# Later batches' scores in four 64 by 64 quarters of the array, with odd chunks reversed and a new order

## The chip, the cores and the metric

One core of a Trainium2 chip runs the program. A time is the device time of one execution in microseconds. TensorE is called PE, VectorE DVE, ScalarE ACT, GpSimd POOL, and SP issues most of the transfers.

## What is computed

A gated linear attention over four batches of eight heads, 768 tokens and 48 features per head, then a Fourier mixing and a feed-forward network (FFN), everything in f32:

```python
for t in range(S):                       # S = 768, per head, D = 48
    state = alpha[t][:, None] * state + outer(k[t], v[t])
    y[t] = q[t] @ state
x = y, heads side by side                # 768 tokens x 384
u = x + real(fft(fft(x, axis=tokens), axis=features))
un = layernorm(u)
out = u + relu(un @ w_ch1) @ w_ch2       # 384 -> 1536 -> 384
```

## The kernel before

**Attention.** Each of the four batches has four pairs of heads (a "unit"). The first head of a pair sits in partitions 0 to 63 (48 used, the rest zero), the second in partitions 64 to 111. The 768 tokens are cut into six chunks of 128. Stage s1 makes running products of the decays by two scans on DVE: A, in a tile of the tag "w3" (printed as w), and its backward counterpart, in the tile al itself. s2 and s3 (`times`) multiply the keys into al and the queries into A. s4 transposes the keys by PE into kt. s5 makes the scores of each chunk: keys as stationary operand, queries as moving operand, so that the output has keys in rows and queries in columns; one matmul per chunk and head, the two heads in the two row halves of the array. A query sees only keys up to its own time, so the lower half of each 128 by 128 block has to be zero. In batch 0 DVE masks while it copies out of PSUM; in batches 1 to 3 (`scores`) ACT copies three chunks at a time to an X tile of the tag w3, and POOL writes the zeros with `affine_select`. The states of the chunks (s6, `states` and `moves`) run on PE, DVE and ACT. s7 (`reads`) multiplies X by the values vn and adds the earlier state's part; two output halves of 64 tokens go to the two column halves of the array. `take` copies the result to y by ACT.

**Mixing, normalising, FFN.** The mixing (folds on DVE, token and feature transforms on PE, a gather of reversed rows through DRAM by POOL) and the normalising give the x tiles. Then an FFN of two blocks per batch runs, each block as 12 slices: nine matmuls of 128x384 into an "f1" bank of PSUM (`mk1`), ACT's relu and DVE's remainder out of it, and nine matmuls into three "f2" banks (`mk2`).

**The order.** The program writes down operations with keys, and a planner (class `Plan`) puts them in order by a model: on each engine the ready operation with the lowest key first. The dictionary `PLACE` replaces single keys by others. An FFN operation is a fill with a late key, so that the attention of batch b+1 goes ahead of the FFN of batch b whenever it is ready. Where the plan leaves PE empty in the first 220 us, warming matmuls on zeros are put in (line 1460, before the change; these are all the records f<-zero). PSUM has three banks "a", two "f1" and three "f2"; there are five w3 tiles, four al tiles and two kq tiles. One scores stage takes three banks a, one bank f1 and two w3 tiles at once. All operations of the plan are recorded by one line, 616, but relu (294) and the warming matmuls (1460).

Of the kernel before, what the change touches and what calls it, by code (L numbers as in the profile page):

```python
# [17 lines left out]
ALU = mybir.AluOpType  # L18
AX = mybir.AxisListType

B, H, S, D = 4, 8, 768, 48
DM = H * D
DFF = 4 * DM
P = 128
NT = S // P
NP2 = H // 2
# [6 lines left out]
GRP = 64  # L33
NV = 64
VW = NT * H // NP2 * D + 32
# [107 lines left out]
THALF = (slice(0, GRP), slice(GRP, P))  # L143
HEADS = ((0, slice(0, GRP)), (1, slice(GRP, CW)))
# [58 lines left out]
def real(x):  # L203
# [5 lines left out]


PLACE = {
# [22 lines left out]
}  # L234


# [17 lines left out]
class Plan:  # L254


    def __init__(self, engines):
        self.engines, self.ops, self.tags, self.direct, self.key, self.chain, self.fill = engines, [], {}, None, 0.0, None, False
        self.idle, self.open, self.both, self.half, self.tight, self.mode, self.run = None, set(), None, None, False, None, None
        self.read, self.last, self.after = {}, None, None  # L260

    def tag(self, name, count, make, reals=None):
        reals = reals or [make(i) for i in range(count)]
# [34 lines left out]
    def add(self, engines, name, args, kwargs):  # L298
# [5 lines left out]
        op = Op(engines, fns, args, kwargs, self.key if self.fill else PLACE.get(round(self.key, 3), self.key))  # L304
        n = len(self.ops)
# [4 lines left out]
        for k, a in named:  # L310
            if isinstance(a, Rows):
                a = a.view
# [10 lines left out]
                    x.tile.uses += 1  # L323
            self.both = None
        op.slots.sort(key=lambda x: x.index if x.tag else -1)
        op.name, op.half, op.mode, op.follows = name, None, None, False
        if name == "matmul":
            p0, p1 = self.region(args[1])[0:2]
            op.half = p0 if p1 - p0 <= GRP else None
# [134 lines left out]
    def emit(self):  # L464
# [35 lines left out]
        while placed < len(ops):  # L500
            placed += 1
            best = None
            for e, cand in wait.items():
# [6 lines left out]
                for n in cand:  # L510
                    op = ops[n]
                    t = start(op, e)
# [18 lines left out]
                n, t = pick  # L531
# [10 lines left out]
            op.engine, op.dur = engine, op.durs[engine]  # L542
            if engine == "PE":
                lead = n + 1 if n + 1 < len(ops) and ops[n + 1].follows else None
                if op.half == GRP and self.half == 0:
                    op.dur = 0.005
                elif op.mode != self.mode:
                    op.dur += max(SWITCH[op.mode], SWITCH[self.mode])
                self.half, self.mode = op.half, op.mode
# [83 lines left out]


@with_exitstack
def gla_mix_ffn(ctx: ExitStack, tc: tile.TileContext, alpha, kq, v, w1, w2, consts, tables, rowtab, out):
    nc = tc.nc
    plan = Plan({"PE": nc.tensor, "ACT": nc.scalar, "DVE": nc.vector, "POOL": nc.gpsimd, "SP": nc.sync})
    V, A, G, T, SY = (Engine(plan, e) for e in ("DVE", "ACT", "POOL", "PE", "SP"))
# [113 lines left out]
    def load_rest(p):  # L753
        if p < B * NP2:
            if p in (2, 3):
                if p == 2:
                    loaded["lent"] = plain(plan.tile("wt11"))
                t = plain(plan.tile(f"wt{7 + p}")).rearrange("p (two s) -> p two s", two=2)
                vn = loaded["lent"][:, (p - 2) * VW : (p - 1) * VW]
            else:  # L760
                t, vn = plan.tile("kq"), plan.tile("vn")
            loaded["kq", p] = t
            loaded["vn", p] = vn
            SY.dma_start(t, kq[p])
            SY.dma_start(vn, v[p, :, 0:VW])

    def setup():
        V.memset(zero, 0.0)
# [53 lines left out]
    def attn_stages(b, hp, i, mixed):  # L822
# [20 lines left out]
            )  # L843

        def R(rows, c):
            return loaded["al", pair][rows, c * CP + 2 : c * CP + 2 + P]

        def Aq(rows, c):
            return e["A"][rows, c * CP + 1 : c * CP + 1 + P]

        def times(which, x, o, c0, c1):
            y = span(x[0:CW], c0, c1, o)
            k = loaded["kq", pair][0:CW, which, c0 * P : c1 * P].rearrange("p (c t) -> p c t", t=P)
            FL["mul"].tensor_mul(y, k, y)

        parts = ((0, 3), (3, NT)) if pair == 0 else ((0, NT),)
# [51 lines left out]
        def scores():  # L908
            tiles = [w3() for _ in range(2)]
            X = [x[:, 0:S].rearrange("p (c n) -> p c n", c=NT) for x in tiles]  # L910
            e["X"] = X
            pc = [[psa() for _ in range(2)], [psa(), plan.tile("f1")]]
            plan.both = pc[0] + pc[1] + tiles
            plan.run = []
            for c in range(NT):
                for hd, r in HEADS:
                    T.matmul(pc[c // 3][hd][:, c % 3 * P : (c % 3 + 1) * P], R(r, c), Aq(r, c), start=True, stop=True)
            plan.run = None
            for h2 in range(2):
                for hd in range(2):  # L920
                    xs = X[hd][:, 3 * h2 : 3 * h2 + 3].rearrange("p c n -> p (c n)")
                    FL["ev"].copy(xs, pc[h2][hd][:, 0:DM])
                    G.affine_select(out=xs, in_=xs, pattern=[[0, 3], [1, P]], compare_op=ALU.is_ge, fill=0.0, base=0, channel_multiplier=-1)

        def s6():
            states()
# [642 lines left out]
def layout(q, k, v, alpha, moe_w_ch1, moe_w_ch2):  # L1569


    def pairs(x, fill):
        t = np.full((B * NP2, P, S), fill, np.float32)
        h = x[:, HORD].reshape(B * NP2, 2, S, D).transpose(0, 1, 3, 2)
        t[:, 0:D], t[:, GRP:CW] = h[:, 0], h[:, 1]
        return t

    decay = np.zeros((B * NP2, P, AW), np.float32)
    decay[..., 0 : NT * CP].reshape(B * NP2, P, NT, CP)[..., 1:] = pairs(alpha, 1.0).reshape(B * NP2, P, NT, P)
    v = v[:, HORD]  # L1580
    v = np.stack([x[..., ::-1] if h >= H // 2 else x for h, x in zip(HORD, v.swapaxes(0, 1))], axis=1)
    values = np.zeros((B * NP2, P, VROW), np.float32)
    values[..., 0 : NT * 2 * D] = v.reshape(B * NP2, 2, NT, P, D).transpose(0, 3, 2, 1, 4).reshape(B * NP2, P, NT * 2 * D)
    return {
        "alpha": decay, "kq": np.stack([pairs(k, 0.0), pairs(q, 0.0)], axis=2), "v": values,
        "w1": np.ascontiguousarray(moe_w_ch1[FEAT]).view(np.int64), "w2": np.ascontiguousarray(moe_w_ch2[:, FEAT]).view(np.int64),
        "consts": dft_constants(), "tables": first_tables(), "rowtab": row_table() - DM,
    }
# [27 lines left out]
```

## Time and profile before

| what | us |
|---|---|
| median of 3 runs (lowest to highest) | 480.93 (478.38 to 482.18) |
| the profiled execution | 478.37 |
| its span, first to last instruction | 476.7 |
| PE busy in it | 468.4 |
| DVE busy | 321.5 |
| ACT busy | 203.0 |
| POOL busy | 53.0 |

The profiled execution lies 1.7 us above its span, and 2.6 us under the median. A matmul's record lasts longer than the time by which it moves the next one on, because matmuls are pipelined: what a stage costs PE is read from the starts, not from the busy time. A matmul with both operands in f32 leaves two records, one in fp32r or a transposition leaves one.

### The profile page before, as it was taken

How to read it: one execution, taken by the hardware profiler on the slowest of the kernel's cores; microseconds unless marked ns; L12 is line 12 of the kernel's file. 1: busy time of each engine (PE TensorE's matmuls, PEld its weight loads, DVE VectorE, ACT ScalarE, POOL GpSimd, SP SyncE). 2: the span in 40 equal slices, each digit the busy share in tenths (PEclk: the TensorE clock that was granted, in tenths of full speed). 3: DMA queues.
4: the chain of work that ended last, by engine and by line, in shares of the span. 5: the costliest groups of instructions: out<-in, count | busy, mean ns of one | idle time of the engine just before them, and what ended most of it. 6: DMA issues, size and time to landing. Idle time of an engine off the chain costs nothing.

```text
span 476.7 us, 10695 instructions
## 1 busy us (share of the span) xinstructions
PE 468.4 (98%) x4546; PEld 444.5 (93%) x4546; DVE 321.5 (67%) x623; ACT 203.0 (43%) x410; POOL 53.0 (11%) x70
## 2 busy tenths in 40 slices
PE   9999999999999999999999999999999999999995
PEld 8979689999999999999999999999999999999994
DVE  7999889999868989657289976583184833113112
ACT  3486759748593234445432254333412251111110
POOL 0000300105113000304120001231130000000000
PEclk9999999999999999999999999999999999999999
DMA  8998215123636201215272001200040001001001
GB/s 304 405 396 322 75 34 191 51 87 133 260 94 180 65 1 51 80 48 194 95 231 77 3 0 51 94 8 22 1 151 1 0 1 51 0 1 50 1 0 56
DMA packets 20981, 46.05 MB, mean 97 GB/s; under 512 B 1920, under 2 KB 11008, under 8 KB 20800
## 3 DMA queue, kind: packets, MB, share of 16 engines
q1 hardware_dynamic: 19872, 42.81, 25.5%
q0 software_dynamic: 768, 2.37, 2.0%
q8 instruction: 37, 0.61, 0.5%
q10 hardware_dynamic: 288, 0.13, 0.1%
q14 instruction: 16, 0.13, 0.1%
HBM read 38.22 MB, written 7.08 MB: 95 GB/s over the span
## 4 chain that ended last, share of the span: by engine, by line
PE 92%; DVE 4%; issue 1%; DMA 1%; ACT 1%; DVEq 0%; ACTq 0%
PE f L616 67%; PE a L616 21%; PE f L1460 4%; DVE al L616 1%; DVE w L616 1%; DVE x L616 1%; DMA al<-in_alpha_dram 1%; DVE tc L616 1%; DVE y L616 0%; ACT b L616 0%; ACT h L294 0%; ACT tt L616 0%; ACT kt L616 0%; DVE back L616 0%; DVE zero L616 0%
## 5 line engine op out<-in xcount | busy, mean ns | idle before, releaser
L616 PE MATMUL f<-wt,h 128*128 128x384 f32 x864 | 173.5, 340 | 0.4 <-ACT h L294 0.4
L616 PE MATMUL f<-x,wt 128*128 128x384 f32 x864 | 171.5, 339 | 0.0
L616 PEld LDWEIGHTS f<-wt,h 128*128 128x128 f32 x864 | 149.4, 188 | 2.6 <-ACT h L294 0.9
L616 PEld LDWEIGHTS f<-x,wt 128*128 128x128 f32 x864 | 150.0, 188 | 1.9 <-issue 0.3
L616 DVE SCALAR_TENSOR_TENSOR h<-f,h 128x384 fp32r<-128x384 f32 x96 | 53.3, 555 | 109.4 <-ACT h L294 108.3
L294 ACT ACTIVATE h<-f 128x384 fp32r<-128x384 f32 x96 | 47.3, 492 | 159.2 <-PE f L616 157.9
L616 POOL TENSOR_SCALAR_AFFINE_SELECT w<-w 128x384 f32<-128x384 f32 x48 | 37.1, 806 | 222.7 <-ACT w L616 222.7
L616 DVE TENSOR_TENSOR y<-y,a 128x191 f32<-128x191 f32 (+3 forms) x65 | 24.5, 427 | 10.4 <-PE a L616 10.2
L616 ACT COPY w<-a 128x384 f32<-128x384 f32 (+4 forms) x48 | 20.7, 484 | 24.8 <-PE a L616 24.6
L616 DVE TENSOR_TENSOR_SCAN al<-al,back 112x773 f32<-112x773 f32 (+1 forms) x17 | 29.7, 1745 | 0.1
L616 DVE TENSOR_TENSOR_SCAN w<-al,d 112x773 f32<-112x773 f32 (+1 forms) x17 | 28.2, 1663 | 0.7 <-DMA al<-in_alpha_dram 0.7
L1460 PEld LDWEIGHTS f<-zero 128*32 128x32 f32 x540 | 25.3, 115 | 3.0 <-issue 1.2
L616 PE MATMUL a<-vn,w 128*64 128x64 f32 x576 | 28.0, 223 | 0.0
L1460 PE MATMUL f<-zero 128*32 128x48 f32 x540 | 26.9, 213 | 1.0 <-DVE zero L616 1.0
L616 PEld LDWEIGHTS a<-vn,w 128*64 128x64 f32 x576 | 25.6, 136 | 0.7 <-issue 0.7
L616 POOL DMA_INDIRECT y<-scr,rows x12 | 15.0, 1247 | 79.3 <-DMA scr<-y 58.0
L616 PE MATMUL a<-tt,w 112*64 112x96 f32 x240 | 22.7, 246 | 0.0
L616 ACT COPY tt<-tc 64x240 f32<-64x240 f32 (+1 forms) x32 | 20.4, 638 | 2.1 <-DVE tc L616 0.9
L616 ACT COPY y<-a 128x288 f32<-128x288 f32 x24 | 9.6, 401 | 26.0 <-PE a L616 25.9
L616 PEld LDWEIGHTS a<-w,al 64*128 64x128 f32 x216 | 16.9, 187 | 3.0 <-issue 2.0
L616 PE MATMUL f<-w,al 48*128 48x128 f32 (+1 forms) x168 | 19.4, 282 | 0.1
L616 PE MATMUL a<-w,al 64*128 64x128 f32 x216 | 19.2, 283 | 0.0
(113 smaller groups left out, 536.6 us busy)
## 6 DMA issues: line engine op xcount, KB each, us to landing
kq<-in_kq_dram SPq DMA_DIRECT2D x13, 768.0 KB, 4.8
wt<-in_w_dram SPq DMA_DIRECT2D x8, 768.0 KB, 12.0
al<-in_alpha_dram SPq DMA_DIRECT2D x15, 388.0 KB, 5.0
out_dram<-y SPq DMA_DIRECT2D x24, 192.0 KB, 3.2
vn<-in_v_dram SPq DMA_DIRECT2D x14, 304.0 KB, 2.9
wt<-in_w_dram SPq DMA_DIRECT2D x8, 384.0 KB
scr<-y SPq DMA_DIRECT2D x4, 577.5 KB
wt<-in_kq_dram SPq DMA_DIRECT2D x2, 768.0 KB
```

The source lines that it names most:

```text
L294: return lambda out, x: e.activation(out, x, AF.Relu)
L616: op.ins = op.fns[op.engine](*[real(a) for a in op.args], **{k: real(x) for k, x in op.kwargs.items()})
L1460: lambda tag, i: nc.tensor.matmul(warm[tag][i][0:32, 512 - FW : 512], zero.real()[:, 0:32], zero.real(), start=True, stop=True), 1.0, WARM,
```

## The change

Only batches 1 to 3 compute otherwise.

- Their scores are made in quarters of the array, 64 rows by 64 columns. An even chunk's first 64 keys go to the left column half and meet all 128 queries; its last 64 keys go to the right half and meet the last 64 queries. In an odd chunk the keys lie in reverse order, so that its last 64 keys are the left 64 columns. Two chunks and two heads then fill the four quarters with 128 queries each, and after that with 64 each. Quarters in which every score would be masked are not computed.
- The host lays out, for those batches, keys and values with the odd chunks reversed (inputs kr and vr), which the loads of kq and vn then read. The product of keys and decays is two DVE operations of three chunks (the odd ones read the decays backwards), and it is written into the kq tile instead of al.
- ACT copies each bank in three pieces: 128 partitions by three chunks of 64 columns, and 64 partitions of one and of two chunks. POOL writes four rectangles of zeros per unit and masks in eight pieces, after all the copies of an X tile.
- In the planner's model three of each four quarter matmuls count 5 ns. `PLACE` is another, for batches 0 and 1; later keys have no entry in it.

```diff
 PLACE = {
-    -700.0: -599.992369, -600.0: -667.427261, -599.99: -599.97122, -599.98: -599.992838, -599.97: -599.992841,
...
+    -700.0: -655.440219, -600.0: -396.201182, -599.99: -599.829417, -599.98: -657.137166, -599.96: 408.044826,
...
 }
...
-                if op.half == GRP and self.half == 0:
+                if op.beside or op.half == GRP and self.half == 0:
                     op.dur = 0.005
...
-            SY.dma_start(t, kq[p])
-            SY.dma_start(vn, v[p, :, 0:VW])
+            SY.dma_start(t, kq[p] if p < NP2 else kr[p - NP2])
+            SY.dma_start(vn, v[p, :, 0:VW] if p < NP2 else vr[p - NP2, :, 0:VW])
...
         def R(rows, c):
+            if b:
+                return loaded["kq", pair][rows, 0, c * P : (c + 1) * P]
             return loaded["al", pair][rows, c * CP + 2 : c * CP + 2 + P]
...
+            if b and which == 0:
+                FL["mul"].tensor_mul(k[:, 0::2], k[:, 0::2], y[:, 0::2])
+                FL["mul"].tensor_mul(k[:, 1::2], k[:, 1::2], y[:, 1::2, ::-1])
+                return
...
-            for c in range(NT):
-                for hd, r in HEADS:
-                    T.matmul(pc[c // 3][hd][:, c % 3 * P : (c % 3 + 1) * P], R(r, c), Aq(r, c), start=True, stop=True)
-            plan.run = None
+            for c0 in range(0, NT, 2):
+                for kh in range(2):
+                    for x in range(2):
+                        c, rows = c0 + x, THALF[kh if x == 0 else 1 - kh]
+                        o = c % 3 * P
+                        for hd, r in HEADS:
+                            plan.beside = x + hd > 0
+                            T.matmul(
+                                pc[c // 3][hd][rows, o + kh * GRP : o + P], R(r, c)[:, rows], Aq(r, c)[:, kh * GRP : P],
+                                start=True, stop=True,
+                            )
+            plan.run, plan.beside = None, False
+            lo, hi = THALF
             for h2 in range(2):
                 for hd in range(2):
-                    xs = X[hd][:, 3 * h2 : 3 * h2 + 3].rearrange("p c n -> p (c n)")
-                    FL["ev"].copy(xs, pc[h2][hd][:, 0:DM])
-                    G.affine_select(out=xs, in_=xs, pattern=[[0, 3], [1, P]], compare_op=ALU.is_ge, fill=0.0, base=0, channel_multiplier=-1)
+                    x, y = X[hd][:, 3 * h2 : 3 * h2 + 3], pc[h2][hd][:, 0:DM].rearrange("p (c n) -> p c n", c=3)
+                    FL["ev"].copy(x[:, :, hi], y[:, :, hi])
+                    for odd, rows in ((0, lo), (1, hi)):
+                        cs = slice((odd + h2) % 2, 3, 2)
+                        FL["ev"].copy(x[rows, cs, lo], y[rows, cs, lo])
+            for x in X:
+                for odd, rows, rest, base, sign in ((0, lo, hi, 0, -1), (1, hi, lo, 1 - P, 1)):
+                    G.memset(x[rest, odd::2, lo], 0.0)
+                    z = x[:, odd::2, hi]
+                    G.affine_select(out=z, in_=z, pattern=[[0, 3], [1, GRP]], compare_op=ALU.is_ge, fill=0.0, base=base + GRP, channel_multiplier=sign)
+                    z = x[rows, odd::2, lo]
+                    G.affine_select(out=z, in_=z, pattern=[[0, 3], [1, GRP]], compare_op=ALU.is_ge, fill=0.0, base=base + (GRP if odd else 0), channel_multiplier=sign)
```

## Rows read from the trace of the kernel before

**Rows 1.** The page's busy times of the engines (busy time, share of the span, x instructions) and, further down, the shares of the chain of work that ended last, by engine.

```profile
PE 468.4 (98%) x4546; PEld 444.5 (93%) x4546; DVE 321.5 (67%) x623; ACT 203.0 (43%) x410; POOL 53.0 (11%) x70
...
PE 92%; DVE 4%; issue 1%; DMA 1%; ACT 1%; DVEq 0%; ACTq 0%
```

**Rows 2.** Busy time of each engine in stretches of 20 us; the columns are the stretch and its length, then for PE, its weight loads, DVE, ACT and POOL the busy time and (x) the instructions, then the granted clock of TensorE as a share of its full 2.4 GHz, the DMA share and GB/s.

```profile
80.00:100.00 20.00, 19.79 (x151) 18.37 (x150) 19.87 (x31) 13.79 (x30) 2.15 (x4) 1.00 0.33 118
100.00:120.00 20.00, 20.00 (x274) 19.00 (x274) 18.94 (x24) 14.55 (x28) 7.02 (x4) 1.00 0.31 101
```

**Rows 3.** The same stretches, the instructions of line 1460 alone, which are the warming matmuls on zeros.

```profile
0.00:20.00 20.00, 14.57 (x284) 14.02 (x284) 1.00 0.91 349
...
60.00:80.00 20.00, 7.79 (x170) 7.38 (x170) 1.00 0.27 82
80.00:100.00 20.00, 0.44 (x6) 0.31 (x6) 1.00 0.33 118
100.00:120.00 20.00, 0.00 (x0) 0.00 (x0) 1.00 0.31 101
```

**Rows 4.** The waits of PE over the whole span: who waited for whom, in total, times, longest.

```profile
PE f L1460 <- DVE zero L616: 1.0, 1, 1.0
PE f L616 <- ACT kt L616: 0.5, 1, 0.5
PE f L616 <- ACT h L294: 0.4, 2, 0.2
```

**Rows 5.** PE's instructions in order of time around the last scores stage of batch 3 and the reads that follow; start, time to the end of the last of the run, and the run's first form (stationary rows*columns, moving operand); a matmul in f32 leaves two records.

```profile
337.62 1.73 PE L616 MATMUL f<-wt,h 128*128 128x384 f32 x9
339.28 1.04 PE L616 MATMUL a<-w,al 64*128 64x128 f32 x13
...
340.49 0.27 PE L616 MATMUL a<-w,al 64*128 64x128 f32 x1
340.50 0.27 PE L616 MATMUL f<-w,al 48*128 48x128 f32 x1
340.61 0.27 PE L616 MATMUL a<-w,al 64*128 64x128 f32 x1
...
340.81 1.83 PE L616 MATMUL f<-x,wt 128*128 128x384 f32 x9
342.48 1.55 PE L616 MATMUL f<-wt,h 128*128 128x384 f32 x8
343.96 0.69 PE L616 MATMUL a<-vn,w 128*64 128x64 f32 x16
344.48 0.34 PE L616 MATMUL a<-tt,w 112*64 112x96 f32 x4
344.65 0.40 PE L616 MATMUL a<-vn,w 128*64 128x64 f32 x8
344.88 0.34 PE L616 MATMUL a<-tt,w 112*64 112x96 f32 x4
```

**Rows 6.** PE's timeline in the last 75 us, where nothing but the FFN's matmuls run.

```profile
405.20 1.72 PE L616 MATMUL f<-wt,h 128*128 128x384 f32 x9
406.76 1.72 PE L616 MATMUL f<-x,wt 128*128 128x384 f32 x9
```

**Rows 7.** Instructions that touch the tile al (in batches 1 to 3 and 0): the records of the scores, their least, median and longest time, first and last start.

```profile
L616 PE MATMUL a<-w,al x216: 270/272/373, 91.0 to 340.6; 64*128 64x128 f32 x108
L616 PE MATMUL f<-w,al x168: 270/272/374, 11.0 to 340.6; 48*128 48x128 f32 x120, 64*128 64x128 f32 x48
```

**Rows 8.** ACT's groups by form: shapes, count, busy time, mean ns of one, idle before it.

```profile
L616 ACT COPY w<-a 128x384 f32<-128x384 f32 x36 | 15.1, 487 | 11.6 <-PE a L616 11.4
...
L616 ACT COPY y<-a 128x288 f32<-128x288 f32 x24 | 9.6, 401 | 26.0 <-PE a L616 25.9
```

**Rows 9.** ACT's timeline after the scores stage of group 5.

```profile
340.24 1.24 ACT L616 COPY w<-a 128x384 f32<-128x384 f32 x3 [1.88 <-PE a L616]
341.36 0.51 ACT L616 COPY w<-f 128x384 f32<-128x384 f32 x1
342.74 0.49 ACT L294 ACTIVATE h<-f 128x384 fp32r<-128x384 f32 x1 [0.87 <-PE f L616]
```

**Rows 10.** POOL's timeline: the longest of the twelve sets of masks, and the last two, undisturbed ones.

```profile
111.45 7.02 POOL L616 TENSOR_SCALAR_AFFINE_SELECT w<-w 128x384 f32<-128x384 f32 x4 [15.77 <-ACT w L616]
...
329.99 1.95 POOL L616 TENSOR_SCALAR_AFFINE_SELECT w<-w 128x384 f32<-128x384 f32 x4 [14.20 <-ACT w L616]
340.79 1.95 POOL L616 TENSOR_SCALAR_AFFINE_SELECT w<-w 128x384 f32<-128x384 f32 x4 [8.86 <-ACT w L616]
```

**Rows 11.** Two of DVE's groups by form: the product of keys and decays over six chunks, and over three.

```profile
L616 DVE TENSOR_TENSOR al<-kq,al 112x768 f32<-112x768 f32 x13 | 13.0, 999 | 0.0
...
L616 DVE TENSOR_TENSOR al<-kq,al 112x384 f32<-112x384 f32 x2 | 1.1, 542 | 0.0
```

**Rows 12.** The chain of work that ended last, its one piece from 388.71 us on.

```profile
388.71 81.15 PE f L616 x468
```

**Rows 13.** PE's groups by form from 388.7 us to the end.

```profile
L616 PE MATMUL f<-wt,h 128*128 128x384 f32 x243 | 46.1, 336 | 0.0
L616 PE MATMUL f<-x,wt 128*128 128x384 f32 x231 | 44.0, 335 | 0.0
```

More of the change, by code (lines that the diff above doesn't have):

```diff
@@ L259, in __init__ @@
         self.idle, self.open, self.both, self.half, self.tight, self.mode, self.run = None, set(), None, None, False, None, None
-        self.read, self.last, self.after = {}, None, None
+        self.read, self.last, self.after, self.beside = {}, None, None, False
     def tag(self, name, count, make, reals=None):
@@ L325, in add @@
         op.slots.sort(key=lambda x: x.index if x.tag else -1)
-        op.name, op.half, op.mode, op.follows = name, None, None, False
+        op.name, op.half, op.mode, op.follows, op.beside = name, None, None, False, self.beside
         if name == "matmul":
@@ L635, in gla_mix_ffn @@
 @with_exitstack
-def gla_mix_ffn(ctx: ExitStack, tc: tile.TileContext, alpha, kq, v, w1, w2, consts, tables, rowtab, out):
+def gla_mix_ffn(ctx: ExitStack, tc: tile.TileContext, alpha, kq, v, kr, vr, w1, w2, consts, tables, rowtab, out):
     nc = tc.nc
@@ L1583, in layout @@
     values[..., 0 : NT * 2 * D] = v.reshape(B * NP2, 2, NT, P, D).transpose(0, 3, 2, 1, 4).reshape(B * NP2, P, NT * 2 * D)
+    turned = values[NP2:].copy()
+    keys = np.stack([pairs(k, 0.0), pairs(q, 0.0)], axis=2)[NP2:]
+    for a in range(1, NT, 2):
+        turned[:, :, a * 2 * D : (a + 1) * 2 * D] = turned[:, ::-1, a * 2 * D : (a + 1) * 2 * D].copy()
+        keys[:, :, 0, a * P : (a + 1) * P] = keys[:, :, 0, a * P : (a + 1) * P][..., ::-1].copy()
     return {
-        "alpha": decay, "kq": np.stack([pairs(k, 0.0), pairs(q, 0.0)], axis=2), "v": values,
+        "alpha": decay, "kq": np.stack([pairs(k, 0.0), pairs(q, 0.0)], axis=2), "v": values, "kr": keys, "vr": turned,
         "w1": np.ascontiguousarray(moe_w_ch1[FEAT]).view(np.int64), "w2": np.ascontiguousarray(moe_w_ch2[:, FEAT]).view(np.int64),
```

41 rows, old and new, of the table PLACE are left out of this document.

## Prediction

> **What bounds the kernel now.** I read the page's busy times first, then a table by stage, the waits, and the timeline around one changed stage. PE is busy for 98% of the span and holds 92% of the chain that ended last [rows 1]. A busy PE alone proves little, because warming matmuls count as busy. They lie almost wholly before 80 us: 14.6 us of them in the first 20 us, 7.8 between 60 and 80, 0.4 between 80 and 100, none later [rows 3]. So there are two regimes. Up to about 80 us PE waits for others and is fed zeros. From there to the end it has useful work without a break: its three longest waits for another engine come to 1.9 us in the whole span, 1.0 of them for the zeros at the start [rows 4]. DVE is as full as PE between 80 and 100 us (19.87 of 20), nearly so until 120 [rows 2], but PE does not wait for it there. The granted clock is 1.00, the 2.4 GHz level, in these stretches [rows 2]. After 80 us, then, PE's time is what counts: time taken off PE there comes off the end, as long as the FFN (the filler) never runs out before the next batch's input is there.
>
> All twelve changed scores stages lie in this second regime: batches 1 to 3 have twelve units, each with 12 matmuls, 24 records. The two groups of their records count 384, 16 units of 24 with batch 0's four; those into a banks start at 91.0 us [rows 7].
>
> **The scores on PE.** In rows 5 an undisturbed run of nine FFN matmuls takes 1.56 us from start to start (406.76 minus 405.20) [rows 6], 0.1735 us each. The nine that start at 337.62 would let the next start at 339.18. The scores start at 339.28: 0.10 us for the change of the array's form. Their last records start at 340.61, and the FFN comes at 340.81, where 0.11 us of a step were still due: 0.09 us lost on the way out. The FFN's first nine then take 1.67 us (342.48 minus 340.81), 0.11 more than 1.56, the weights that could not be loaded ahead. In between, the two heads' records step together: from 339.28 to 340.61 are 1.33 us, less 0.10 for the first weight load, over 11 steps: 0.112 us (340.49 to 340.61 is one). Twelve steps are 1.34 us. The stage costs 0.10 + 0.10 + 1.34 + 0.09 + 0.11 = 1.74 us.
>
> The new stage has, for each two chunks, four matmuls of 128 columns at once and then four of 64. No row shows a quarter. The nearest are the row halves above, where 128 columns take 0.112 us a record, and the column halves of the reads: eight records of 64 columns, in pairs, take 0.23 us (344.88 minus 344.65), 0.058 a pair [rows 5]. Both are the streaming time and about 5 ns. If the four quarters run at once, two chunks take 2 x 0.112 + 2 x 0.058 = 0.34 us in place of 0.448, the stage 1.02 in place of 1.34. The first load has 64 columns rather than 128 and shrinks from 0.10 to about 0.05; the ways in and out stay. That is 1.74 to 1.37, **0.37 us a unit, 4.4 us in twelve**. The bounds: with only two quarters at once, two chunks take 0.68 and a unit 2.04, which is 0.65 more than now after the smaller load, 7.8 us lost; at best the ways out shrink too (the last pass is 0.05 shorter), 0.42 a unit, 5.0 us gained. I take 4.4, since the row halves and the column halves each run side by side in the rows, within 10 ns of each other's starts (340.49 and 340.50).
>
> **The copies on ACT.** Now four copies of 384 columns, 487 ns each; one of 288 takes 401 [rows 8], so a column costs 0.9 ns and an instruction 143 ns. Pieces of 192, 128 and 64 columns are then about 315, 258 and 200 ns, 773 against 487: four sets are 3.1 us. But copies overlap: three take 1.24 us and the whole train ends at 341.87, 1.63 us after it began [rows 9]. So the new train takes between 1.63 (only columns count) and 3.1 us, 0 to 1.5 us longer. ACT is 43% busy [rows 1], so the sum of some 14 us more of instructions costs nothing by itself. What counts is the f1 bank, which the last copy frees, and relu, which stands behind copies in ACT's queue. After the stage of rows 5 PE runs nine matmuls into the other f1 bank and eight of the second half until 343.96; the scores' bank was free at 341.9, so 2.1 us of cover stand against 1.5. If the new order leaves less, PE waits up to 1.5 us a unit, 18 us in twelve. I take **0.5 us in all**, near the lower end, because the cover seen is larger than the longest addition; both ends stay in the range only so far as the chain's rival reaches.
>
> **The masks on POOL.** Four masks of 384 columns take 1.95 us undisturbed, 7.02 at the worst, while DVE is full [rows 10]. Now eight masks of 192 and four fills: a mask is between 0.25 us (half) and 0.49 (the same). The fills wait for no copy. All eight masks of a unit wait for both copies of their head, so after the last copy there are 1.6 to 3.5 us of masks where one mask of 0.49 stood: the reads can start 1 to 3 us later by POOL and 0 to 1.5 by ACT. PE has the FFN for this: there are 3.35 us between the last scores record and the reads now (340.61 to 343.96), filled with 17 FFN matmuls. It costs nothing while filler is left.
>
> **DVE and the transfers.** The split product is 2 x 542 instead of 999 ns [rows 11], 0.085 us twelve times, 1 us of DVE beside a PE that does not wait for it: nothing, at most 1 us. The backward read is not in the trace; I take it like the forward one. al is free earlier and kq later, after the scores instead of after the query product; kr and vr are as large as what they replace, on the same queue. SP's queue takes them in order, and a later kq delays the load of the unit two further on, which is a unit's length away: nothing.
>
> **The new order.** PLACE decides the first 80 us, where DVE works on batch 0 and PE is warmed. I cannot work out a term from the keys. The warming matmuls of 60 to 80 us, 7.8 us [rows 3], are what a better order could at most win, and as much could be lost. I take 0 and a width of 2.5 us either way.
>
> **Sum.** 478.4 (the profiled execution) - 4.4 + 0.5 = 474.5. The median of the runs shown is 480.9, 2.5 above that execution, so on the median's scale the forecast is **477.0 us**, 0.8% less.
>
> **The rivals.** *The records bound the stage, not the streams.* The densest stretch in rows 5 has eight records in 0.23 us, 29 ns each. If this is what PE can take in, 48 records cost 1.39 us, and a stage that had 1.34 gains only at its edges: nothing on PE, 480.9 + 0.5, say 481. For it: nothing in the rows is denser. Against it: the two records of a pair start 10 ns apart, and the 64-column step is explained by its stream. A page of the Trainium skill has a rule of this kind: TensorE: Matmul & The Clock Gate, "Wait — 56ns, not 53.3ns?", puts a floor of about 25 ns on start to start, however few the columns. By it 48 records would be 1.2 us and the gain 0.19 a unit, 2.3 us in all; the trace neither reaches that floor on average nor excludes it. The Trainium skill's TensorEngine Tiling (Array Packing), Instruction Overhead, warns not to take a tile from a dimension that is already small, since a matmul has some 60 cycles of overhead; that speaks against the 64-column passes, and the 0.058 us a pair in the rows does not show such an addition for two tiles. No run here shows it for four.
>
> *The chain becomes the bound: slower.* There are five w3 tiles; a unit holds one for A and two for X until its reads, the next unit's A a fourth, so the next scores wait for the reads before them. A later read thus adds up over four units. At the end 474 FFN matmuls stand after the last other work [rows 12, 13], of which one batch has 432: 42 x 0.1735 = 7.3 us of batch 2's filler were left. It decides from 7.3 / 4 = 1.8 us a unit. My two ranges together give 1 to 4.5. Where all of it adds up at 4.5, PE idles 18 - 7.3 = 10.7 us: 480.9 - 4.4 + 10.7 = 487. Against it: the last two sets of masks start 10.8 us apart [rows 10], while the scores to reads take 4.7 (339.28 to 343.96), so not all is chained. More likely half adds up, and then it costs up to 2 us: 479.
>
> *Two quarters at a time: slower.* The change then doesn't do what it says: 480.9 + 7.8 + 0.5 = 489. It decides where a group of four takes over 1.3 times 0.34 us.
>
> **How the numbers follow.** Forecast 0.56, between 474 and 480 with the order's width. Records as bound 0.15, around 479 to 482. The chain 0.16, half of it under 482 and half up to 487. Two at a time 0.05. A first phase that moves by more than 2.5 us, 0.04 each way: under 473.5, or over 483. The range 472.5 to 484 leaves out two at a time, the upper part of the chain's and a piece of both ends, under 2 in 10. One per cent is 4.8 us, about what a measurement can tell from no change: faster by more means under 476.1. From the forecast 0.31, from a better first phase 0.04: 0.35. Slower by more means over 485.7: two at a time 0.05, the chain's upper half 0.04, the first phase 0.01: 0.10. The rest is 0.55.
>
> **What would show it.** Right: 576 score records with 64 columns of weights, a unit's from first to last start in about 1.0 us instead of 1.33; no PE wait over 1 us after 90 us; the same 1.56 us cadence in the FFN's tail, only earlier by 4 us. Records as bound: about 0.2 us for each group of eight, also with 64 columns. The chain: PE waiting for POOL's w or for x tiles at a batch's end. The order: another sum of warming matmuls, and the first FFN matmul earlier or later. The prediction is wrong most easily in what it doesn't price, the first 80 us.

## The result and the profile after

The changed kernel takes 483.18 us (median of 12 runs, 482.28 to 485.58) against 480.61 for the kernel before (12 runs, 478.38 to 482.77): a ratio of 1.0056, 95% interval 1.0033 to 1.0079. It is slower by half a per cent; 477.0 us and a gain had been forecast. Between the lowest runs of the two the distance is 3.9 us; the kernel before has executions some 3 us longer in which the granted clock fell (last section). The profiled execution took 482.35 us, its span 480.5.

The page's busy times and shares of the chain that ended last, which answer to [rows 1]:

```profile
PE 466.5 (97%) x4770; PEld 439.3 (91%) x4770; DVE 317.0 (66%) x628; ACT 214.4 (45%) x513; POOL 62.5 (13%) x166
...
PE 88%; ACT 5%; DVE 4%; issue 1%
```

PE's busy time fell, yet the span grew by 3.8 us. ACT has 11.4 us more, and 5% of the chain where it had 1%. PE's waits, which answer to [rows 4] (who waited for whom, in total, times, longest):

```profile
PE a L615 <- ACT w L615: 3.3, 10, 0.4
PE f L1483 <- DVE zero L615: 1.1, 1, 1.1
PE f L615 <- ACT h L293: 1.0, 2, 0.8
PE f L615 <- ACT kt L615: 0.9, 3, 0.5
PE a L615 <- ACT x L615: 0.8, 1, 0.8
```

The first line is new: ten waits of a score matmul for an ACT copy of scores. This view counts only the time in which no record of PE runs; what the waits cost is worked out from the starts below. By form they are all on one kind of quarter (records of the new stage; the last column is the idle time before them and its releaser):

```profile
L615 PE MATMUL a<-w,kq 64*64 64x128 f32 x144 | 14.8, 280 | 0.0
L615 PE MATMUL a<-w,kq 64*64 64x64 f32 x144 | 12.1, 223 | 3.3 <-ACT w L615 3.3
```

PE's timeline in the last unit of batch 3 shows where they lie (start, time to the end of the run of records, first form):

```profile
345.87 0.67 PE L615 MATMUL a<-w,kq 64*64 64x128 f32 x19
...
346.39 0.27 PE L615 MATMUL f<-w,kq 48*64 48x128 f32 x1
346.93 0.38 PE L615 MATMUL a<-w,kq 64*64 64x64 f32 x4 [0.28 <-ACT w L615]
...
347.50 0.21 PE L615 MATMUL f<-w,kq 48*64 48x64 f32 x1
347.65 0.44 PE L615 MATMUL f<-wt,h 128*128 128x384 f32 x1
```

and ACT's timeline beside it:

```profile
346.67 0.32 ACT L615 COPY w<-a 64x64 f32<-64x64 f32 x2 [0.46 <-PE f L615]
347.29 1.07 ACT L615 COPY w<-a 128x192 f32<-128x192 f32 x5 [0.30 <-PE a L615]
```

The reader sees a knot. Chunk 1's single piece (64 partitions by 64 columns) is complete after the first two chunks, so the plan puts its two copies, one per head, into the order amid the stage. The bank they read is still being filled. In the program's order the copies come after the 128-column quarter of chunk 2 and before its 64-column quarter. So the copy waits for the group of records that starts at 346.37 (its last, into f, starts at 346.39) and begins at 346.67; the next quarter into that bank waits for the copy, though the two touch different columns, and starts at 346.93. Groups that would follow each other in 0.11 us are 0.56 apart.

Two of the twelve units have no such copy inside. Here is one of them, the first of batch 3:

```profile
297.60 0.67 PE L615 MATMUL a<-w,kq 64*64 64x128 f32 x19
...
298.20 0.21 PE L615 MATMUL a<-w,kq 64*64 64x64 f32 x1
...
298.61 0.22 PE L615 MATMUL f<-w,kq 48*64 48x64 f32 x1
298.76 0.61 PE L615 MATMUL f<-wt,h 128*128 128x384 f32 x2
```

From first to last start it takes 1.01 us (297.60 to 298.61), where the stage of [rows 5] took 1.33 and the disturbed one 1.63.

Worked out from the starts of PE's records, in the way of the prediction (from the cadence of the FFN before it to the cadence behind it), a stage cost 1.74 us before. Undisturbed it costs 1.365 now, disturbed 1.93 to 2.03. The twelve sum to 20.9 us before and 22.8 after: 16.4 for the work and 6.4 for the ten waits.

The rest of the 3.7 us between the last FFN matmul's starts (470.6 before, 474.3 after) lies in the main in batch 1, between 93 and 158 us. There PE's time for FFN matmuls grew by 1.5 us and for the transpositions of the keys by 0.9, with fewer warming matmuls against it (0.4). One such place, PE behind the transpositions:

```profile
96.64 0.64 PE L615 MATMUL a<-cst,kq 112*128 112x112 f32 x5
98.12 1.31 PE L615 MATMUL f<-wt,h 128*128 128x384 f32 x6 [0.84 <-ACT h L293]
```

and what stood in ACT's queue before that relu:

```profile
91.90 1.04 ACT L615 COPY w<-a 128x192 f32<-128x192 f32 x4
92.84 0.50 ACT L293 ACTIVATE h<-f 128x384 fp32r<-128x384 f32 x1
93.22 1.20 ACT L615 COPY w<-a 64x128 f32<-64x128 f32 x5
94.45 0.71 ACT L615 COPY w<-f 128x192 f32<-128x192 f32 x3
95.18 1.32 ACT L615 COPY tt<-tc 64x240 f32<-64x240 f32 x2
96.53 0.94 ACT L615 ACTIVATE b<-al,cm 112x768 uint8<-112x768 uint8 x1
...
97.58 0.49 ACT L293 ACTIVATE h<-f 128x384 fp32r<-128x384 f32 x1
```

From 91.90 ACT has no gap until the relu at 97.58.

### The profile page after: what moved, and what is told of

It is laid out like the page before. It is cut to its first block, busy times and chain, and to the rows that moved or that the text cites. A ratio compares the mean times of both kernels' runs of the same rounds, so it can differ in the third digit from the quotient of the medians.

```text
span 480.5 us, 11414 instructions
## 1 busy us (share of the span) xinstructions
PE 466.5 (97%) x4770; PEld 439.3 (91%) x4770; DVE 317.0 (66%) x628; ACT 214.4 (45%) x513; POOL 62.5 (13%) x166
## 4 chain that ended last, share of the span: by engine, by line
PE 88%; ACT 5%; DVE 4%; issue 1%
PE f L615 65%; PE a L615 20%; PE f L1483 3%; ACT w L615 1%; ACT b L615 1%; ACT tt L615 1%; DVE tc L615 1%; DVE wt L615 1%; DVE y L615 1%; DVE w L615 1%; ACT wt L615 1%; DVE z L615 0%; ACT h L293 0%; DVE st L615 0%; DVE h L615 0%
## 5 line engine op out<-in xcount | busy, mean ns | idle before, releaser
L615 POOL TENSOR_SCALAR_AFFINE_SELECT w<-w 128x192 f32<-128x192 f32 x96 | 35.7, 394 | 149.0 <-ACT w L615 146.6
L615 ACT COPY w<-a 128x192 f32<-128x192 f32 (+6 forms) x120 | 28.0, 286 | 22.9 <-PE a L615 13.2
L615 DVE TENSOR_TENSOR_SCAN al<-al,back 112x773 f32<-112x773 f32 (+1 forms) x17 | 28.3, 1666 | 0.1
L1483 PEld LDWEIGHTS f<-zero 128*32 128x32 f32 x476 | 23.1, 117 | 3.7 <-DVE zero L615 1.1
L1483 PE MATMUL f<-zero 128*32 128x48 f32 x476 | 25.1, 216 | 1.4 <-DVE zero L615 1.1
L615 POOL DMA_INDIRECT y<-scr,rows x12 | 13.5, 1124 | 80.1 <-DMA scr<-y 68.2
L615 DVE TENSOR_TENSOR y<-y,f 128x384 f32<-128x384 f32 x30 | 15.7, 552 | 10.1 <-PE f L615 10.1
L615 PEld LDWEIGHTS a<-w,kq 64*64 64x64 f32 (+1 forms) x432 | 13.7, 132 | 8.7 <-ACT w L615 5.7
L615 POOL MEMSET w<- 64x192 f32 x48 | 12.2, 254 | 71.2 <-PE a L615 69.5
```

The costliest lines, as they stand in the source:

```text
L615: op.ins = op.fns[op.engine](*[real(a) for a in op.args], **{k: real(x) for k, x in op.kwargs.items()})
L1483: lambda tag, i: nc.tensor.matmul(warm[tag][i][0:32, 512 - FW : 512], zero.real()[:, 0:32], zero.real(), start=True, stop=True), 1.0, WARM,
```

## Experiments

**Tie all copies behind the stage.** The first attempt to take the ten waits away.

```diff
+            last = plan.run[-1]
             plan.run, plan.beside = None, False
...
+            def ev(out, x):
+                FL["ev"].copy(out, x)
+                plan.ops[-1].deps.add(last)
...
-                    FL["ev"].copy(x[:, :, hi], y[:, :, hi])
+                    ev(x[:, :, hi], y[:, :, hi])
...
-                        FL["ev"].copy(x[rows, cs, lo], y[rows, cs, lo])
+                        ev(x[rows, cs, lo], y[rows, cs, lo])
```

> The kernel after with one tie more in the plan: ACT's copies of a scores stage come after the stage's last matmul in the order. Theory W (a copy placed inside the run of quarters makes the next quarters wait, ten times, 0.55 to 0.66 us each): the stage is 1.02 us from first to last start in all twelve units, the twelve stages cost 12 x 1.37 = 16.4 us instead of 22.8, and the time falls by about 6.4 us from 483.2, to about 476.8, a ratio to the kernel before of 0.992. Rival O (the new order and the longer chain behind the scores cost the time, the waits stand where PE had to wait anyway): the waits reappear after the stage, as waits for POOL's masks or for a bank, and the time stays within 2 us of 483.

Measured: 486.77 us, ratio 1.0131 (1.0102 to 1.0160). The stage did what theory W says: 1.017 us from first to last start in all twelve units, 16.4 us in sum. The total went the other way. The tie made the planner write another order for the whole kernel. PE's timeline and two stretches of the table by stage:

```profile
137.45 1.32 PE L615 MATMUL f<-x,wt 128*128 128x384 f32 x6 [0.32 <-ACT w L615]
140.96 1.33 PE L615 MATMUL f<-x,wt 128*128 128x384 f32 x3 [2.19 <-ACT wt L615]
```

```profile
130.00:140.00 10.00, 8.45 (x88) 7.50 (x86) 7.22 (x15) 6.30 (x17) 3.45 (x7) 1.00 0.24 80
140.00:150.00 10.00, 8.80 (x105) 7.69 (x109) 5.38 (x9) 5.20 (x10) 1.11 (x4) 0.66 0.11 33
```

PE waited 2.2 us for weights that are split late, and the granted clock fell: 0.66 on average between 140 and 150 us. From 185.2 us on, all 432 FFN matmuls of batch 0 were done, and PE got 28 records of warming matmuls. At the end no filler was left over: behind the last other PE work stand just one batch's FFN matmuls, 432, and one more (the view takes in one that began earlier), and PE had no wait there:

```profile
L615 PE MATMUL f<-wt,h 128*128 128x384 f32 x218 | 41.8, 336 | 0.0
L615 PE MATMUL f<-x,wt 128*128 128x384 f32 x216 | 41.0, 335 | 0.0
```

So this run tells what the stage costs, but not what the waits cost the kernel: two things were changed at once.

**The same with the old table of keys.**

```diff
 PLACE = {
-    -700.0: -655.440219, -600.0: -396.201182, -599.99: -599.829417, -599.98: -657.137166, -599.96: 408.044826,
+    -700.0: -599.992369, -600.0: -667.427261, -599.99: -599.97122, -599.98: -599.992838, -599.97: -599.992841,
...
 }
```

> As the run with the copies after the stage, but with the table of keys of the kernel before. Theory W with the remaining 1.8 us put down to the new order (stalls of batch 1 between 93 and 158 us): 480.6 - 4.5 = about 476.1, no PE stall over 0.4 us after 90 us, some 1.5 us under the run with the new table. If the remaining stalls come from the three-piece copies: the same as that run, within 0.7 us, with stalls of PE on ACT in batch 1.

Measured: 498.29 us, ratio 1.0381 (1.0340 to 1.0422). Again 1.017 us a stage; but PE got 886 records of warming matmuls instead of the 476 of the changed kernel, 352 of them after 90 us, where useful work was late. Of these, 326 stand between 160 and 200 us, 15 us of PE's time: all 432 FFN matmuls of batch 0 were done at 173.2 us. That is the kind of loss that the rival of the chain describes, a filler that runs out. But it lies behind batch 1 and not at the end, and the table of keys is all that differs from the run above; that the chain of the w3 tiles would do it is not shown.

**The new table on the code before.** The diff is the table alone, in the other direction.

> The kernel before with the new table of keys alone. If the new order costs the stalls of batch 1: 480.6 + 1.8 = about 482.4. If they come from the copies in pieces: 480.6 within 0.7. That the new order wins time in the first 80 us and the quarters lose more than shown would give under 479.

Measured: 487.45 us, ratio 1.0105 (1.0055 to 1.0155, four runs). Behind the first FFN matmul the profiled execution takes 404.7 us to the last one, 399.6 before: 5 us of stalls in batch 1 and in its mixing. The median fits none of the three expectations. But the profiled execution had the dip of the clock in the first phase too (last section), with its first FFN matmul at 74.2 us instead of 70.9, and the lowest of the four runs, 482.29 us, lies at the first expectation: four runs do not price the order well. A table of keys fits the code for which it was made, and the order of one kernel cannot be priced on another.

**Hold every order, undo only the knot.** After the plan is made, the matmuls of a stage are drawn together in the program's order. Each engine's own sequence of instructions stays the same.

```diff
+        for run in self.runs:
+            i, rest = order.index(run[0]), set(run[1:])
+            order = [x for x in order[: i + 1]] + run[1:] + [x for x in order[i + 1 :] if x not in rest]
         self.order = [n for n in order if isinstance(n, int)]
...
+            plan.runs.append(plan.run)
             plan.run, plan.beside = None, False
```

> The kernel after with every engine's own order kept to the instruction; only in the program's order are the matmuls of one scores stage drawn together ahead of the copies that stood between them, so that none of them has to wait for a copy. Theory W: all twelve stages take 1.02 us from first to last start, the ten waits (6.4 us) go, and as no order moves, they come off the end: 483.2 - 6.4 = about 476.8, ratio to the kernel before 0.992. Rival C (what PE gains in the stage it loses right behind it, in waits for a bank, relu or the masks): 481 to 483, with as many microseconds of new PE waits between the scores and the reads.

Measured: 478.36 us (11 runs, 476.07 to 480.46), ratio 0.9943 (0.9915 to 0.9970). That is faster than both kernels. The waits of PE, and the stage that had the knot above:

```profile
PE f L618 <- ACT h L293: 1.1, 2, 0.9
PE f L1487 <- DVE zero L618: 1.1, 1, 1.1
PE f L618 <- ACT kt L618: 0.9, 3, 0.5
PE a L618 <- ACT x L618: 0.8, 1, 0.8
PE f L618 <- DVE h L618: 0.5, 1, 0.5
```

```profile
341.43 0.67 PE L618 MATMUL a<-w,kq 64*64 64x128 f32 x19
...
342.44 0.22 PE L618 MATMUL f<-w,kq 48*64 48x64 f32 x1
342.59 0.79 PE L618 MATMUL f<-wt,h 128*128 128x384 f32 x3
```

All ten waits for copies are gone; of the others, those for ACT and for the zeros stay as they were, and one for DVE (the last line shown) is new. The last FFN matmul starts at 469.2 us instead of 474.3: 5.1 of the 6.4 us that were taken out of the stages come off the end. In ratios it is 1.13% between the two kernels, 5.4 us. Theory W holds; rival C took about 1 us of it: a stall of 0.85 us at 128.6 us that the changed kernel did not have. That is the new wait, and DVE's timeline shows what stood before the remainder h that PE waited for:

```profile
129.40 0.62 PE L618 MATMUL f<-wt,h 128*128 128x384 f32 x2 [0.51 <-DVE h L618]
```

```profile
128.32 0.56 DVE L618 TENSOR_TENSOR kq<-kq,al 112x384 f32<-112x384 f32 x1 [1.37 <-DMA kq<-in_kr_dram]
128.80 0.55 DVE L618 SCALAR_TENSOR_TENSOR h<-f,h 128x384 fp32r<-128x384 f32 x1
```

The product of keys and decays waited 1.37 us for the load of kr, and the remainder stood behind it in DVE's queue.

**Lengthen ACT's train by 0.85 us a unit.**

```diff
                         FL["ev"].copy(x[rows, cs, lo], y[rows, cs, lo])
+                        plan.ops[-1].twice = (odd + h2) % 2 == 1
...
+            if getattr(op, "twice", False):
+                op.fns[op.engine](*[real(a) for a in op.args], **{k: real(x) for k, x in op.kwargs.items()})
             op.ins = op.fns[op.engine](*[real(a) for a in op.args], **{k: real(x) for k, x in op.kwargs.items()})
```

> As the run with the stage's matmuls drawn together, but each copy of 64 partitions by one chunk is done twice, 48 more ACT copies of 0.21 us, 0.85 us more of ACT per unit (10.2 us in all), in the same order. If ACT's train has cover in most units: under 2 us slower than the run without the repeats, and where it loses it is in batch 1. If the train sits on PE's path: 5 us and more slower.

Measured: 484.51 us, ratio 1.0103 (1.0067 to 1.0139), 6.1 us over the run without the repeats. Of 10.2 us more on ACT, six reach the end. The waits show by which way:

```profile
PE f L620 <- ACT w L620: 2.4, 6, 0.7
PE f L620 <- ACT h L293: 2.3, 4, 1.5
```

Six waits of an FFN matmul for a copy of scores are waits for the f1 bank that the stage holds: three in batch 1, two in batch 2, one in batch 3. ACT is idle for more than half the span, and yet in six of the twelve units its train behind the scores has less than 0.85 us of cover left.

**Shorten ACT's queue by 1.12 us a unit.** The range check of the decays is left out of batches 1 to 3, in the run with the stage drawn together and in the kernel before.

```diff
                 check(pair, span(loaded["al", pair], 0, NT, 0))
+                plan.ops[-1].skip = b > 0
...
+            if getattr(op, "skip", False):
+                continue
             for slot in op.slots:
```

> As the run with the stage's matmuls drawn together (ratio 0.9943), with 1.12 us of ACT left out per unit of batches 1 to 3: the range check of the decays (one activation of 0.94 us and the read of its sum), 13.5 us in all; every other instruction and every order as there. This leaves out the guard for extreme decays, not a part of the output for these inputs. Theory A (PE's remaining stalls of batch 1, about 2.6 us, come from ACT's queue, which three-piece copies made longer): the stalls at 97, 128 and 143 us shrink by half or more and the ratio falls to about 0.990. Rival P (they come from the places that the new table gave the operations): the same stalls, ratio 0.993 to 0.995.

> The kernel before with the same check left out. There PE waited 0.4 us for relu in the whole span, so ACT has cover and the time stays within 0.3% under theory A and under rival P; a gain over 0.5% would mean that ACT was on PE's path before the change already.

Measured: 476.89 us, ratio 0.9942 (0.9923 to 0.9962), for the first, and 479.00 us, ratio 0.9996 (0.9975 to 1.0018), for the second. In the total the first is no different from the run without the omission (0.9943). PE behind the transpositions in its profile:

```profile
97.03 0.64 PE L620 MATMUL a<-cst,kq 112*128 112x112 f32 x5
97.78 1.32 PE L620 MATMUL f<-wt,h 128*128 128x384 f32 x6
```

The gap there is 0.36 us from start to start where it was 1.14, so this stall was ACT's queue, as theory A has it. The stalls at 128 and 143 us stayed (0.87 and 0.76 us from start to start, 0.85 and 0.77 without the omission), as rival P has it. From the first score of batch 1 to the last FFN matmul it is 377.0 us instead of 378.4; the runs do not resolve that. What PE waits for in the two stalls that stayed can be read: at 128 us for DVE, as above, behind a late load of kr. At 143 us (in the run with the check) relu stands in ACT's queue behind an operation that waits 1.14 us for DVE, which waits for the weights' cast on ACT, and that cast stands behind the twelve copies of the stage. Whether the new places or the longer train make this second one is not tested. The kernel before does not gain, as both expected.

## Why the prediction was wrong

**The quarters: right to 0.01 us.** The term of 0.37 us a unit, 4.4 us in twelve, was worked out from row halves and column halves. The drawn-together run measured 1.365 us a stage against 1.74: 0.375, 4.5 us. Four quarters run at once with the cadence of two halves. That the records bound the stage is refuted: 48 records take 1.02 us, 21 ns each, under the 29 ns of the densest stretch in [rows 5]. The Trainium skill (TensorE: Matmul & The Clock Gate, "Wait — 56ns, not 53.3ns?") puts a floor of about 25 ns from start to start; the trace goes under it, and the measurement decides here. Two quarters at a time is refuted by the same number.

**The copies: the step that failed.** The prediction's term for them, 0.5 us in all, counted what ACT's train costs behind the stage, through the f1 bank, and in its queue, before relu. PE's wait for a copy inside the stage stood at nothing, without a reason. It did not ask what a smaller piece can do that a whole bank's copy could not: be ready while the stage still runs. The old copy of a bank needed all three chunks of it, so it could only follow them; a piece of one chunk is complete before the bank is. The cost was in the diff: three copies per bank, each with its own point of readiness, from a bank that later quarters write. It is 6.4 us for ten units, more than the gain of 4.5, and drawing the stage together gave 5.1 of them back. That 483.2 us still lies in the range given, 472.5 to 484, is luck: the upper part of that range stood for the rivals and the first phase, and none of them made the loss. Adding a wait should have been asked of PE, not of ACT alone: who reads a bank that PE has not finished?

**ACT's cover: the second miss, smaller.** The sizes were right: the pieces measured 320, 262 and 212 ns where 315, 258 and 200 had been worked out. The groups after, answering to [rows 8]:

```profile
L615 ACT COPY w<-a 128x192 f32<-128x192 f32 x36 | 11.3, 320 | 2.6 <-PE a L615 2.4
...
L615 ACT COPY w<-a 64x128 f32<-64x128 f32 x36 | 9.4, 262 | 1.1 <-PE a L615 0.8
...
L615 ACT COPY w<-a 64x64 f32<-64x64 f32 x36 | 6.9, 212 | 9.1 <-PE f L615 8.9
```

But 2.1 us of cover had been read from one unit of batch 3 [rows 9], where ACT had nothing else to do, and carried to all twelve. In batch 1 the same queue holds the checks and the states' copies [rows 2], and PE stalls there cost about 2 us more than before, where 0.5 were forecast for the kernel. One of the stalls is shown to be ACT's queue; not all are. The loads, too, had been put at nothing: in the changed kernel DVE waits 4.6 us in four waits for kr, none of which reaches PE, and with the knot undone one of them does, at 128 us.

**POOL and the chain: right.** A mask is 416 or 373 ns (0.25 to 0.49 forecast). The masks' groups:

```profile
L615 POOL TENSOR_SCALAR_AFFINE_SELECT w<-w 128x192 f32<-128x192 f32 x48 | 20.0, 416 | 147.4 <-ACT w L615 146.6
L615 POOL TENSOR_SCALAR_AFFINE_SELECT w<-w 64x192 f32<-64x192 f32 x48 | 17.9, 373 | 1.6
```

The last unit's reads start 6.5 us after its scores (345.87 to 352.36) instead of 4.7, and the filler held: 473 FFN matmuls stand behind the last other work, where [rows 13] had 474. The rival of the late chain did not decide this kernel. In the first two experiments the filler did run out, though through the order, so the question was not idle.

**The order: right at zero where it was priced.** The first FFN matmul starts at 71.1 us (70.9 before), the first scores of batch 1 at 90.98 us in both kernels. The warming matmuls of 60 to 80 us, against [rows 3]:

```profile
60.00:80.00 20.00, 6.68 (x144) 6.28 (x144) 1.00 0.26 80
```

Whether the remaining stalls of batch 1 belong to the new order or to the new work can't be told apart: the two other orders that carry the same work, those of the first two experiments, have larger stalls of their own.

With the knot undone the kernel runs at 478.4, and by the ratio at 477.9 on the scale of the 480.6, where 477.0 was forecast. That this is close does not make the rest of the sum right. In the profiled executions the time from the first FFN matmul to the last is 399.6 us before and 398.2 with the knot undone: of the 4.5 us taken out of the stages 1.4 reach the end, and the stalls of batch 1 take most of the rest. The sum was missing one large term and had a smaller one too low.

## What to carry to other kernels

When a copy out of PSUM is cut into pieces, list for each piece the instruction that completes it, and see whether the producer still writes to the same bank behind that point; if so, keep the producer's instructions together in the program's order; here that took all ten waits away. Read an engine's cover in the stage where its queue is fullest, not in the quietest one. And where an order is generated, test one cause with every engine's sequence held fixed: a single added tie made the total 3.6 us longer while the stage itself gained the 6.4 us that were expected.

## What the runs showed of the hardware

Four 64 by 64 quarters in f32 run side by side without a loss against two halves: 48 records in 1.02 us, with steps of 0.11 us for 128 columns, as for the row halves of [rows 5].

A stall can come with a loss beyond its length. In the first experiment a wait of PE of 2.2 us from 138 us on came with about 6.8 us at the 1.2 GHz level of the clock (the stretch shown there has 0.66 on average, and 6.8 us at half speed with 3.2 us at full speed make 0.66). The granted clock also falls in the first phase of some executions. This is the profiled execution of the kernel before without its checks:

```profile
20.00:30.00 10.00, 9.75 (x182) 8.47 (x181) 10.00 (x15) 7.94 (x18) 0.00 (x0) 1.00 1.05 393
30.00:40.00 10.00, 9.40 (x132) 7.98 (x129) 9.00 (x20) 7.62 (x12) 0.00 (x0) 0.83 1.03 401
40.00:50.00 10.00, 9.94 (x184) 9.48 (x181) 8.83 (x20) 5.05 (x10) 0.00 (x0) 0.83 0.54 206
```

The granted clock is 0.83 in two stretches, and the first FFN matmul comes at 74.3 us instead of 70.9. PE was busy 9.75 of 10 us in the stretch before the fall and 9.40 in the next. In the profiled execution of the kernel before, where the clock stayed at 1.00, it was 9.76 and 9.46; these busy times do not tell the two apart, and what makes the clock fall here is open. All three stretches lie ahead of the first instruction that this run leaves out, so such a dip belongs to the kernel before as well, whose times spread from 478 to 483 us.
